# Scheduling a two-layer linear-attention and Mish kernel as one block on a more detailed timing simulator

## The chip, the cores and the metric

The kernel runs on one NeuronCore of a Trainium2 chip. Its time is the device time of one execution in microseconds, and a version is judged by the median of its runs. The engines are called as in the profile: PE is TensorE's matmul stream and PEld its weight loads, DVE is VectorE, ACT is ScalarE, POOL is GpSimd, and SP is the engine whose queue issues every DMA of this kernel.

## The reference

The input x has 2048 tokens of 640 features, in float32. Two layers are run one after the other with the same weights. Each layer has two parts, and each part adds its result to x:

```
x = x + A(layernorm(x))     # linear attention, 32 heads of 20 features
x = x + B(layernorm(x))     # dense 640 -> 1536, Mish, dense 1536 -> 640
x = x + A(layernorm(x))
x = x + B(layernorm(x))

A:  q, k, v = split(x @ wqkv)
    phi(z) = concat(softmax(z @ w_phi), softmax(-z @ w_phi))        # per head
    o = phi(q) @ (phi(k)^T v) / (phi(q) . sum_s phi(k) + 1e-6)
    return o @ wo
B:  h = x @ w1 + b1
    return (h * tanh(softplus(h))) @ w2
```

The sums over all tokens in phi(k)^T v separate each attention part into a first pass, which makes the sums, and a second pass, which uses them.

## The kernel before

Tokens are worked in 8 blocks of 256, each of two tiles of 128. Every large product is made in three passes of float32 matmuls: weights and activations are each cut into a high part (rounded to 12 bits) and the low rest, and high by high, high by low and low by high are summed in PSUM. The cut of a weight (`split`, L123 to L125) is a DMA into the staging tile `st`, of which there are two, a rounding copy on ScalarE (L124) and a subtraction (L125) on GpSimd or, for the values' weights, on VectorE.

Per layer there are three stages.

- `attend_first`: for each tile the products for keys, queries and values (`project`, L293), the softmax features in stages spread over ScalarE, VectorE and GpSimd (L314 to L325), the store of phi(q) to DRAM (L367), and the sums phi(k)^T v (L359). The next block is normalized and transposed meanwhile: `Transposed.step` makes transposes on TensorE (L252), a rounding copy on ScalarE and a subtraction on VectorE (L258).
- `attend_second`: phi(q) is loaded (L463) and transposed (L477); the transposes leave PSUM by ScalarE (L483) or VectorE (L481); the averages are made (L498) and divided (L507 to L511); they are transposed (L252) and multiplied by wo (L293), and the result is added to x (L518). In between, W1 and half of W2 are loaded and split.
- `dense`: a step takes 256 hidden features of one block: `hidden` makes 30 matmuls (L569) into one PSUM tile named `one`, `mish` runs its elementwise chain L582 to L595 over ScalarE and VectorE with its last subtraction on GpSimd (L595), and `contract` adds 24 matmuls (L611) into two PSUM tiles named `mm`. The trace order is skewed by two: `hidden` of step i comes before `contract` of step i - 2. A block has six steps; at a block's end `end` adds the result to x (L629). Near a block's end the next block's three transpose steps are traced around the last `hidden`.

PSUM holds four `one` tiles and two `mm` tiles. All five engines run queues in order; they wait for one another by semaphores.

The order in each queue is made at compile time. The framework runs the traced program through a timing simulator; whenever an engine can take an instruction in the simulation, it gets the ready one that was traced earliest, and PSUM and SBUF buffers are handed out in the same run. The chip then keeps that order, whatever the real times are. The kernel binds this choice in a few places: most ScalarE instructions outside `mish`, `split` and the transposes' copies are chained into trace order by a helper, and a few loads are told to be issued behind a named instruction. For instance:

```
def act(*args, **kw):
    ...
        with tc.issue_after(last_act[0]):
            ins = nc.scalar.activation(*args, **kw)
```

The framework has two timing simulators. The one in use before is the simpler one.

Of the kernel before, what the change touches and what calls it, by code (L numbers as in the profile page):

```python
# [16 lines left out]
P = 128  # L17
S = 2048
D = 640
F = 1536  # L20
H = 32
DH = 20
KD = D // P
KF = F // P
BT = 2
# [17 lines left out]
def kernel(  # L43
# [28 lines left out]
    def big_tile():  # L72
        return work.tile([P, EW], F32, tag="big", name="big", bufs=5)
# [7 lines left out]
    def row_block(t, b):  # L81
        return t[b * BLK:(b + 1) * BLK, :].rearrange("(p t) d -> p t d", t=BT)

    # constants
    ident = const.tile([P, P], F32, name="ident")
    make_identity(nc, ident)
    b1s = const.tile([P, KF], F32, name="b1s")
# [1 line left out]
    nc.vector.memset(neg_half, -0.5)  # L89
    two = const.tile([P, 1], F32, name="two")  # L90
    nc.vector.memset(two, 2.0)
    # per group of three heads: the block diagonal of phi_k^T [v | 1], by pairs of groups
    kvb = const.tile([120, GP, P], F32, name="kvb")
    # rstd and -mean*rstd of every token, for the next layer norm
    stats = const.tile([P, NB, 2, BT], F32, name="stats")

    # spills
    wp_d = dram.tile([2, 2, KD, P, D], F32, name="wp_d")
    e_d = dram.tile([NT, P, EW], F32, name="e_d")
    x1_d = dram.tile([S, D], F32, name="x1_d")  # L100
# [2 lines left out]
    last_act = [None]  # L103

    def act(*args, **kw):
        """An activation that ScalarE issues after the one before it in this order."""
        if last_act[0] is None:
            ins = nc.scalar.activation(*args, **kw)
        else:
            with tc.issue_after(last_act[0]):  # L110
                ins = nc.scalar.activation(*args, **kw)
        last_act[0] = ins.ins

# [1 line left out]
    def v_tile():  # L115
        return work.tile([P, VW], F32, tag="v", name="v", bufs=2)

# [9 lines left out]
    def r1_pair(k):  # L127
        return tuple(wts.tile([P, F], F32R, tag=f"r1{s}{k}", name=f"r1{s}{k}") for s in "hl")
# [8 lines left out]
        return tuple(wts.tile([P, D], F32R, tag=f"r2{s}{j}", name=f"r2{s}{j}") for s in "hl")  # L137

    def load_v_weights():
        """R1 holds [Wk' | Wv] by chunks of rows; the values' part."""  # L140
        ws = [r1_pair(k) for k in range(KD)]
        for k in range(KD):
            split(ws[k][0][:, D:2 * D], ws[k][1][:, D:2 * D], wv[k * P:(k + 1) * P, :], D, nc.vector,
                  (None, None, v_tile, v_tile, big_tile)[k])
        return ws
# [31 lines left out]
        return ws  # L177

    def load_w2(fs):
        """Rows of W2 by tiles of hidden features; the last five go where Wo was."""  # L180
        ws = {}
        for f in fs:
            ws[f] = r2_pair(f if f < 5 else (f + 5 if f < 7 else f - 2))
            split(ws[f][0], ws[f][1], w2[f * P:(f + 1) * P, :], D, nc.gpsimd)
        return ws

    def load_raw(which):
        """W's transpose, queries' or keys' part, by chunks of six heads."""
        raw = []
        wide = r2_wide(10 + which, F32)  # L190
        for t in range(6):
            rows = 120 if t < 5 else 40
            if t < 5:
                r = wts.tile([P, D], F32, tag=f"r2{'hl'[which]}{5 + t}", name=f"raw{which}{t}")
            else:
                r = wide[:, 0]
            nc.sync.dma_start(r[:rows], wqk_t[which * D + t * 120:which * D + t * 120 + rows, :])
            raw.append((r, rows))
        return raw

    def fold_phi(ws, bd, raw):
        """W' = W . blockdiag(w_phi), from W's transpose."""
        for k in range(KD):
            if k % 2:
                ps = [one_tile(), one_tile()]
            else:
                ps = mm_tile()
                ps = [ps[:, 0], ps[:, 1]]
            for t in range(6):
                r, rows = raw[t]  # L210
                nc.tensor.matmul(ps[t // 3][:, (t % 3) * 120:(t % 3) * 120 + rows],
                                 r[:rows, k * P:(k + 1) * P], bd[:rows, t, :rows],
                                 start=True, stop=True)
            hi, lo = ws[k][0][:, :D], ws[k][1][:, :D]
            for c, (a, b) in enumerate(((0, 360), (360, D))):
                nc.scalar.activation(hi[:, a:b], ps[c][:, :b - a], AF.Copy)
                nc.vector.tensor_tensor(lo[:, a:b], ps[c][:, :b - a], hi[:, a:b].bitcast(F32),
                                        op=ALU.subtract)

# [1 line left out]
    def norm_stats(t, xt):  # L221
        """Mean and variance of a tile's tokens."""
        bn = work.tile([P, 2, 6], F32, tag="bn", name="bn", bufs=4)
        for c in range(2):
            nc.vector.bn_stats(bn[:, c], xt[:, t, c * HC:(c + 1) * HC])
        mv = work.tile([P, 2], F32, tag="mv", name="mv", bufs=4)
        nc.vector.bn_aggr(mv, bn)
        return mv

    def norm_scale(b, mvs):  # L230
        """stats[:, b] = rstd, -mean*rstd."""
        ve = work.tile([P, BT], F32, tag="ve", name="ve", bufs=4)
        for t in range(BT):
            nc.gpsimd.tensor_scalar(ve[:, t:t + 1], mvs[t][:, 1:2], LN_EPS, 1.0, op0=ALU.add, op1=ALU.mult)
        nc.gpsimd.tensor_tensor(stats[:, b, 0], ve, neg_half, op=ALU.pow)
        for t in range(BT):
            nc.vector.scalar_tensor_tensor(stats[:, b, 1, t:t + 1], mvs[t][:, 0:1], -1.0,
                                           stats[:, b, 0, t:t + 1], op0=ALU.mult, op1=ALU.mult)

    class Transposed:  # L240
        """A block's rows, transposed: chunks of features by tokens, high and low parts."""

        def __init__(self, rows):
            self.rows, self.hs, self.ls = rows, [], []
# [24 lines left out]
        return work.tile([P, D], F32, tag="xn", name="xn", bufs=2)  # L269

    def normed(b, xt):
        """The normalized block, yet to be transposed."""
        xn = [row_tile() for _ in range(BT)]
        for t in range(BT):
            act(xn[t], xt[:, t, :], AF.Identity,
                                 bias=stats[:, b, 1, t:t + 1], scale=stats[:, b, 0, t:t + 1])
        return Transposed(xn)

# [1 line left out]
    def project(xts, t, ws, col, ps=None):  # L280
        """(tokens of tile t) . w[:, col:col + D], in halves."""
        if ps is None:
            mm = mm_tile()
            ps = [mm[:, 0], mm[:, 1], mm]
# [10 lines left out]
        return ps  # L295

    def both(ps):
        """The two halves as one operand, where they lie in one tile."""
        return ps[2][:, :, :HC]

# [1 line left out]
    def query_tile(i):  # L302
        return r2_wide(10 + i % 2, F32).rearrange("p s d -> p (s d)")

    def features(ps, e, pool_sub):
        """Softmax of both signs, [head, sign, feature], in stages."""
        eg = e.rearrange("p (g d) -> p g d", d=DH)
        eh = e.rearrange("p (h s d) -> p s h d", s=2, d=DH)
        act(e.rearrange("p (c h s d) -> p s c h d", c=2, s=2, d=DH)[:, 1],
# [18 lines left out]
    def fetch(x_src, b, xt=None):  # L328
        xt = x_tile() if xt is None else xt
        nc.sync.dma_start(xt, row_block(x_src, b))  # L330
        return xt

    def attend_first(layer, x_src, first):
        """Sums phi_k^T [v | 1] over all tokens; spills phi_q."""

        def fetch_normed(b):
            xt = fetch(x_src, b)
# [94 lines left out]
        return kva, kvz, o_ws, advance  # L432

    def finish_kv(kva, kvz, mask):
        """The block diagonals of the sums, features on partitions, by pairs of groups."""
        acc, acz = (work.tile([P, D], F32, tag="st", name="st", bufs=2) for _ in range(2))
        for src, dst, p1, n, w in ((kva, acc, P, 4, 120), (kvz, acz, P, 1, 120), (kvz, acz, 42, 1, 80)):
            c = 120 if w == 80 else 0
# [14 lines left out]
    def attend_second(x_src, x_dst, acc, at, begin_next):  # L453
# [11 lines left out]
            return ins  # L465

        def features_t(b):
            """phi_q transposed, by pairs of groups of three heads."""
            es = loaded.pop(b)
            phs = []  # L470
            for m in range(6):
# [13 lines left out]
            return phs  # L485

        def averages(phs):
            """phi_q . phi_k^T v over phi_q . sum(phi_k), a block's rows."""
            os_ = []
            for t in range(BT):  # L490
                po = mm_tile()
# [59 lines left out]
                at(b)  # L551
        return nxt

# [1 line left out]
    def dense(x_src, x_dst, w1s, w2s, first, last):  # L555
        blocks = {0: first}
        exps = [None]
# [17 lines left out]
            return ah, al  # L575

        def mish(pr, js, ph, ta, tb, ah, al):
            """n = e^h (e^h + 2); mish = h n / (n + 2)"""
            part = lambda t, c: t[:, c * 512:(c + 1) * 512].rearrange("p (f s) -> p f s", f=2)[:, js]
            e, n, r, m = part(ta, 0), part(ta, 1), part(tb, 0), part(tb, 1)  # L580
            for j in range(js.start, js.stop):
# [88 lines left out]
                    end(b)  # L670
        return nxt, kv_ws

    src, first = x, None
    for layer in range(LAYERS):
        last = layer == LAYERS - 1
        dst = out if last else x2_d
        acc = attend_first(layer, src, first)
        if layer == 0:
            nc.sync.dma_start(b1s, b1)
        w1s = []  # L680
        w2s = {}

        def at(b):
            if b < KD:
                w1s.append(r1_pair(b))
                split(w1s[b][0], w1s[b][1], w1[b * P:(b + 1) * P, :], F, nc.gpsimd)
            else:
                w2s.update(load_w2(((0, 1, 2), (3, 4), (5, 6))[b - KD]))

        x1t = []  # L690

        def begin_dense():
            x1t.append(fetch(x1_d, 0, big_tile().rearrange("p (t d) -> p t d", t=BT)))
            return normed(0, x1t[0])

        begun = attend_second(src, x1_d, acc, at, begin_dense)
        first = dense(x1_d, dst, w1s, w2s, [x1t[0], begun, None], last)
        src = dst


# [36 lines left out]
```

## Time and profile before

| | |
|---|---|
| median of 3 runs | 1491.22 us (1490.75 to 1491.38) |
| span of the profiled execution | 1497.6 us |
| TensorE matmul busy | 1461.3 us, 98%, 12100 matmuls |
| VectorE busy | 985.0 us, 66% |
| ScalarE busy | 623.8 us, 42% |
| GpSimd busy | 455.7 us, 30%, 360 instructions |
| DMA | 135.37 MB, mean 90 GB/s |

The profile is of one execution, and no other time of that execution is given than its span, which is 6.4 us (0.4%) above the median of the runs. Busy times are taken from the span's records. In the chain of waits and in the groups, "A <- B" says that instruction A waited last for instruction B. In the tables of stretches, PEclk is the share of TensorE's full clock that was granted in that stretch.

### The profile page before, as it was taken

What the parts mean: (1) busy time and instruction counts of PE and PEld (TensorE: products, weight loads), DVE (VectorE), ACT (ScalarE), POOL (GpSimd) and SP (SyncE); (2) the same over time, 40 slices, a digit from 0 to 9 for tenths busy, and PEclk for the clock granted to TensorE, in tenths of its full rate; (3) what the DMA queues carried; (4) which work ended last, traced back from release to release, by engine and by line L of the source; (5) the groups of instructions that cost most, each with busy time, mean ns of one, the idle gap of its engine ahead of it and who ended that gap; (6) DMA issues with size and microseconds to landing.
All of it is one profiled execution on the core that took longest, in us unless ns stands there. A gap on an engine that the chain in (4) does not pass through costs nothing.

```text
span 1497.6 us, 28601 instructions
## 1 busy us (share of the span) xinstructions
PE 1461.3 (98%) x12100; PEld 1438.8 (96%) x12100; DVE 985.0 (66%) x1734; ACT 623.8 (42%) x1051; POOL 455.7 (30%) x360
## 2 busy tenths in 40 slices
PE   7999999999999999999989999999999999999998
PEld 7999999898999999999989999998999999999998
DVE  5787767655577667666659566675656776666665
ACT  4534343523354444444444344333334444444443
POOL 1554434424042222122144334352332212111111
PEclk9999999999999999999999999999999999999999
DMA  8521113665310110001441112136562000000100
GB/s 264 198 76 54 71 62 117 219 234 199 116 45 18 36 36 31 7 36 36 161 174 71 54 54 88 55 109 251 206 202 89 10 18 37 36 36 36 36 2 36
DMA packets 39586, 135.37 MB, mean 90 GB/s; under 512 B 4777, under 2 KB 6313, under 8 KB 39457
## 3 DMA queue, kind: packets, MB, share of 16 engines
q1 hardware_dynamic: 39457, 133.53, 25.2%
q8 instruction: 95, 1.56, 0.4%
q14 instruction: 34, 0.28, 0.1%
HBM read 85.02 MB, written 48.50 MB: 89 GB/s over the span
## 4 chain that ended last, share of the span: by engine, by line
PE 80%; DVE 7%; DMA 4%; ACT 3%; POOL 2%; issue 1%; SPq 0%; DVEq 0%; ACTq 0%; POOLq 0%
PE mm L293 33%; PE one L569 19%; PE mm L611 19%; PE one L252 3%; DMA st<-in_w 3%; PE one L359 3%; PE one L477 2%; DVE big L593 1%; PE mm L498 1%; DVE big L585 1%; DVE big L584 1%; DVE big L592 1%; POOL r2l L125 1%; DVE big L591 1%; ACT big L586 1%
## 5 line engine op out<-in xcount | busy, mean ns | idle before, releaser
L611 PE MATMUL mm<-r2h,ol 128*128 128x320 f32 x1280 | 304.7, 311 | 6.2 <-POOL ol L595 5.2
L595 POOL TENSOR_TENSOR ol<-big,ol 128x512 fp32r<-128x512 f32 (+1 forms) x98 | 129.7, 1324 | 494.2 <-ACT ol L594 386.9
L569 PE MATMUL one<-xtl,r1h 128*128 128x256 f32 x960 | 271.8, 283 | 1.0 <-DVE xtl L258 1.0
L569 PE MATMUL one<-xth,r1h 128*128 128x256 f32 x960 | 272.7, 284 | 0.0
L569 PE MATMUL one<-xth,r1l 128*128 128x256 f32 x960 | 271.6, 283 | 0.0
L611 PEld LDWEIGHTS mm<-r2h,ol 128*128 128x128 f32 x1280 | 221.2, 190 | 7.3 <-POOL ol L595 6.0
L293 PE MATMUL mm<-r2h,xth 128*128 128x320 f32 x640 | 202.2, 316 | 0.0
L611 PE MATMUL mm<-r2l,ol 128*128 128x320 f32 x640 | 198.8, 311 | 0.0
L293 PE MATMUL mm<-r2h,xtl 128*128 128x320 f32 x640 | 198.2, 310 | 0.0
L293 PE MATMUL mm<-r2l,xth 128*128 128x320 f32 x640 | 198.2, 310 | 0.0
L293 PE MATMUL mm<-r1h,xth 128*128 128x320 f32 x600 | 188.8, 315 | 0.0
L293 PE MATMUL mm<-r1h,xtl 128*128 128x320 f32 x600 | 185.4, 309 | 0.0
L293 PE MATMUL mm<-r1l,xth 128*128 128x320 f32 x600 | 185.3, 309 | 0.0
L569 PEld LDWEIGHTS one<-xtl,r1h 128*128 128x128 f32 x960 | 183.9, 192 | 1.4 <-DVE xtl L258 1.4
L569 PEld LDWEIGHTS one<-xth,r1l 128*128 128x128 f32 x960 | 184.2, 192 | 0.0
L569 PEld LDWEIGHTS one<-xth,r1h 128*128 128x128 f32 x960 | 183.8, 191 | 0.0
L584 DVE TENSOR_SCALAR big<-big 128x512 f32<-128x512 f32 (+1 forms) x98 | 56.2, 574 | 162.1 <-ACT big L582 157.9
L594 ACT ACTIVATE ol<-big 128x512 fp32r<-128x512 f32 (+1 forms) x98 | 61.0, 623 | 199.0 <-DVE big L593 198.9
L325 POOL TENSOR_TENSOR r<-r,r 128x1280 f32<-128x1280 f32 x32 | 75.7, 2365 | 155.4 <-DVE r L324 154.0
L586 ACT ACTIVATE big<-big,two 128x512 f32<-128x512 f32 (+1 forms) x98 | 70.0, 715 | 125.9 <-DVE big L585 123.8
L293 PEld LDWEIGHTS mm<-r2h,xth 128*128 128x128 f32 x640 | 120.8, 189 | 0.8
L611 PEld LDWEIGHTS mm<-r2l,ol 128*128 128x128 f32 x640 | 121.4, 190 | 0.0
(107 smaller groups left out, 2937.8 us busy)
## 6 DMA issues: line engine op xcount, KB each, us to landing
e_d<-r SPq DMA_DIRECT2D x32, 640.0 KB, 3.2
big<-e_d SPq DMA_DIRECT2D x32, 640.0 KB, 6.4
xt<-x_d SPq DMA_DIRECT2D x30, 640.0 KB, 4.0
x_d<-xt SPq DMA_DIRECT2D x23, 640.0 KB, 2.9
st<-in_w SPq DMA_DIRECT2D x44, 320.0 KB, 3.8
xt<-in_x SPq DMA_DIRECT2D x16, 640.0 KB, 5.0
out<-xt SPq DMA_DIRECT2D x6, 640.0 KB, 2.9
st<-in_wo SPq DMA_DIRECT2D x10, 320.0 KB, 3.0
```

What stands on the lines that cost most here:

```text
L125: eng.tensor_tensor(lo[:, c0:c1], st, hi[:, c0:c1].bitcast(F32), op=ALU.subtract)
L252: nc.tensor.transpose(ps[:, c, t * P:(t + 1) * P], self.rows[t][:, (c0 + c) * P:(c0 + c + 1) * P], ident)
L293: nc.tensor.matmul(ps[c][:, :HC], l[:, sl], r, start=(n == 0), stop=(n == 3 * KD - 1))
L325: nc.gpsimd.tensor_tensor(eg, eg, r.unsqueeze(2).to_broadcast([P, 2 * H, DH]), op=ALU.mult)
L359: nc.tensor.matmul(acc[64 * n:64 * n + m, c:c + w], v[:, GW * g:GW * g + m], e[:, 120 * g:120 * g + w], start=(i == 0 and p in (0, 4)), st ...
L477: nc.tensor.transpose(ps[:rows, n, t * P:(t + 1) * P], es[t][:, 120 * g:120 * g + rows], ident)
L569: nc.tensor.matmul(ph[:, j, :], l, r, start=(n == 0), stop=(n == 3 * KD - 1))
L584: nc.vector.tensor_scalar_min(e, e, E_CAP)
L586: nc.scalar.activation(r, n, AF.Ln, bias=two)
L594: nc.scalar.activation(ah[:, js], n, AF.Copy)
L595: nc.gpsimd.tensor_tensor(al[:, js], n, ah[:, js].bitcast(F32), op=ALU.subtract)
L611: nc.tensor.matmul(pys[t][:, c, :HC], l[:, j, sl], r, start=(f == 0 and n == 0), stop=(f == KF - 1 and n == 2))
```

## The change

The two-layer loop is put inside a block of its own, and the block is marked to be scheduled with the more detailed of the framework's two timing simulators. The setup ahead of it (the identity, two small constants, the table preload and the declarations of buffers) stays outside and is scheduled as before. What is traced in the block is scheduled as a unit, and nothing outside is mixed in. By the framework's description of the option, the simpler simulator leaves out the fixed cost of GpSimd's elementwise instructions, which the detailed one has. No instruction is added, removed or resized, and no buffer count changes. Comments and docstrings are taken out as well.

```
-    src, first = x, None
-    for layer in range(LAYERS):
-        last = layer == LAYERS - 1
-        dst = out if last else x2_d
-        acc = attend_first(layer, src, first)
...
-        begun = attend_second(src, x1_d, acc, at, begin_dense)
-        first = dense(x1_d, dst, w1s, w2s, [x1t[0], begun, None], last)
-        src = dst
+    with tc.block(schedule_with_timeline_sim=True):
+        src, first = x, None
+        for layer in range(LAYERS):
+            last = layer == LAYERS - 1
+            dst = out if last else x2_d
+            acc = attend_first(layer, src, first)
...
+            begun = attend_second(src, x1_d, acc, at, begin_dense)
+            first = dense(x1_d, dst, w1s, w2s, [x1t[0], begun, None], last)
+            src = dst
```

## The prediction

> **What bounds the kernel now.** I read the page's busy times first, then TensorE's list of waits, then ScalarE's, then the order of time around each long wait. The page:
>
> ```profile
> span 1497.6 us, 28601 instructions
> PE 1461.3 (98%) x12100; PEld 1438.8 (96%) x12100; DVE 985.0 (66%) x1734; ACT 623.8 (42%) x1051; POOL 455.7 (30%) x360
> ```
>
> TensorE does the same 12100 matmuls after the change, so the change can only move the 36.3 us of the span in which no matmul is busy, and what clock is lost around them. TensorE's waits (line, what it waited for, total us, times, longest):
>
> ```profile
> PE mm L211 <- DMA raw<-in_wqk_t: 7.6, 1, 7.6
> PE one L252 <- DVE xn L511: 6.5, 14, 2.9
> PE mm L611 <- POOL ol L595: 5.2, 3, 4.2
> PE one L477 <- ACT ol L483: 4.2, 3, 2.5
> PE one L252 <- DVE big L589: 3.8, 2, 1.9
> PE mm L611 <- DVE big L629: 1.0, 1, 1.0
> PE one L569 <- DVE xtl L258: 1.0, 2, 0.5
> ```
>
> With 2.5 us in smaller rows the list holds 31.8 us; the other 4.5 us is nearly all the end after the last matmul. The 7.6 us is the first load and the end is the last store; no order removes them. That leaves 24.2 us. Two stretches then run at half clock, which the stretches show (columns: stretch, length, busy times, PEclk, DMA):
>
> ```profile
> 1024.50:1027.00 2.50, 2.50 (x10) 2.50 (x11) 1.50 (x6) 0.42 (x1) 0.92 (x2) 0.50 0.60 171
> 759.00:764.00 5.00, 5.00 (x19) 5.00 (x20) 0.52 (x1) 0.74 (x1) 2.00 (x2) 0.50 0.02 8
> ```
>
> The second follows a gap of 4.56 us from matmul to matmul (at 754.25); 21 matmuls took some 267 ns in place of 147, which costs 21 x 0.12 = 2.5 us. The first follows a gap of 3.12 us at 1021.39; its 30 matmuls of one product took 5.81 us where others take 4.64, so 1.2 us. A gap of 2.78 us at 359.99 was followed by none. The pool that any order can win is thus 24.2 + 3.7 = 27.9 us, 1.9% of the time. Whoever looks for a larger gain must find it outside TensorE's waits, and there is nothing there.
>
> **The steady stretches.** From 468 to 740 us and from 1200 to 1480 us TensorE never pauses. In step 20 of the first dense stage GpSimd's L595 ends at 557.88 and its matmul starts at 563.66: 5.8 us in hand. The two L595 forms take 0.723 us (shortest, 256 elements) and 1.296 us (median, 512), so 2.2 ns an element and about 0.15 us fixed (an estimate from these two). The description says that the simpler simulator omits just this fixed cost; all 360 instructions together make 54 us by it, but 0.15 us against 5.8 us moves no order there. I cost the steady stretches at nothing; the cover is those 5.8 us, and were it gone, each of some 90 steps would pay its excess. What can change lies at the transitions.
>
> **The change part by part.** It adds, removes and resizes no instruction. It moves them in their queues, SP's DMAs included, and it opens a block.
>
> *The block's entry.* No jump shows in this trace. Bound: zero if each engine runs straight on; one instruction packet if it must fetch, and 95 packets on the instruction queue took 0.4% of 16 engines' span, so 1.0 us each. SP issues the first load at 0.72 us and TensorE's first matmul waits for loads, so nothing hides it. I take the middle, +0.5. The Trainium skill (Runtime: NRT & Kernel Launch, Instruction fetch mechanics) says that a taken branch to code outside the fetched window stalls for that fetch; by it the term would be +1.0. No jump is in this trace to test it.
>
> *Weight copies at the head of ScalarE.* ScalarE's waits:
>
> ```profile
> ACT r1h L124 <- DMA st<-in_w: 72.5, 23, 8.0
> ACT r2h L124 <- DMA st<-in_w: 26.3, 10, 8.5
> ```
>
> and the order of time on ScalarE around 360 (start, length, in brackets the idle time before and what ended it):
>
> ```profile
> 360.41 0.74 ACT L124 ACTIVATE r2h<-st 128x640 fp32r<-128x640 f32 x1 [3.22 <-DMA st<-in_w]
> 362.14 2.04 ACT L483 ACTIVATE ol<-one 120x512 f32<-120x512 f32 x4
> ```
>
> The simulated order put L124 where its load should have landed; on the chip it had not, and ScalarE stood 3.2 us with four ready L483 behind it. TensorE's L477 then waited 2.5 us for a PSUM tile. The same shape stands at 1099 (1.5 us) and at 1018.9 to 1020.8, where a waiting L124 holds back an xth copy and TensorE loses 2.9 us and 1.2 us of clock. A simulator that times DMAs more closely would let the chain go first: 4.0 + 4.1 = 8.1 us gone. What is late next is L124, by one or two copies of 0.74 us; its weights are used a stage later.
>
> *A transpose ahead of ready matmuls.* At 435.95 TensorE stands before the last two L252 of the next block, which wait for a PSUM tile until L589 has read it:
>
> ```profile
> 435.95 0.28 PE L569 MATMUL one<-xth,r1l 128*128 128x256 f32 x1
> 438.13 0.44 PE L252 MATMUL one<-ident,xn 128*128 128x128 f32 x2 [1.90 <-DVE big L589]
> 438.32 1.12 PE L611 MATMUL mm<-r,ol 128*128 128x320 f32 x6
> ```
>
> The 24 matmuls L611 behind them were ready: their L595 ended at 436.16. Chosen by real readiness they go first, and L252 falls into them. Again at 1173.85. Gone: 3.8 us, and the 1.0 us that L569 then waits for L258. In the wait for L629 (1.0 us) I see no ready work for certain, and leave it.
>
> *The end of the first layer.* The 4.25 us before L611 at 754.56 come from L595:
>
> ```profile
> L595 POOL TENSOR_TENSOR ol<-big,ol x98: 723/1296/4906, 412.7 to 1489.9; 128x512 fp32r<-128x512 f32 x94, 128x256 fp32r<-128x256 f32 x4
> ```
>
> (Of GpSimd's L595: shortest, median and longest in ns.) The shorter form takes 0.723 us elsewhere and 4.906 us here, at 753.85, while VectorE runs eight instructions with two inputs nearly without pause (five splits L125 and three of `mish`). The Trainium skill (SBUF — State Buffer, Summary: rules for kernel authors) says that a VectorE instruction with two SBUF inputs and a GpSimd instruction exclude one another until the first ends. By that rule L595 would wait for one of them (0.83 us) and not for all; a scheduler that follows it believes L595 done by 755.4, keeps TensorE's order, and the gap stays; the trace disagrees with the rule, since all eight went first. If instead values' matmuls (L293) are drawn into the gap, 4.25 + 2.5 = 6.8 us go. I take 0, the value of today's row, and keep 6.8 for the range.
>
> *The rest.* Thirteen waits for L511 in the second pass make 3.6 us without the long one; both `mm` tiles are then held by the averages, so they stay.
>
> *New waits.* A greedy order tuned by another clock makes its own mistakes: hand-set chains stay while their neighbours move. Nothing in the trace prices them but today's mistakes of the same sort: 8.1 + 4.8 = 12.9 us. Bounds: 0 and about twice that; I take half, 6.5.
>
> Sum: 0.5 - 8.1 - 4.8 + 6.5 = -5.9 us. Against the span that gives 1491.7; the profiled span stands 6.4 us above the median, so 1485.3 for the median (0.4% faster).
>
> **Rivals.** *Tiles taken by running ahead* (slower). If the new order draws `hidden` ahead whenever `contract` isn't ready, the four `one` tiles fill, and the next block's transposes wait at each block end as they do at two of fourteen inside the dense stages today, for 1.9 + 0.5 = 2.4 us each. At ten more ends it costs 24 us, and with the 8.1 won (the 4.8 are not) and 0.5 for the entry that is +16.4: 1507.6. It decides from four ends, where it outweighs the 8.1. For it: the tiles are held for a whole `mish` chain. Against it: 5.8 us in hand in the steady state. Chance 0.39, with smaller forms down to 1495.
>
> *No change that shows.* The order in the large stretches is bound by PSUM tiles and data, and the two corrections are eaten by new mistakes: 0.5 - 12.9 + 12.9, so 1491.7. Chance 0.13. (A measurement of this kernel tells 0.2%, 3 us, from no change.)
>
> *The layer's end filled as well.* -5.9 - 6.8 = -12.7: 1478.5. Chance 0.14, part of faster.
>
> *The option does little because the simulators agree.* It falls together with the second rival, since the queue order would be the same.
>
> **How the numbers follow.** Forecast -5.9 has 0.34, the filled end 0.14: faster 0.48. Same 0.13. Slower 0.39. Low end: everything won and no new waits would be 0.5 - 12.9 - 6.8 = -19.2, so 1472.0; I stop at 1475. High end: the first rival at ten ends, 1507.6, so 1508. The likeliest case's own range is 1478 to 1490.
>
> **What would show it.** Right: the waits of L477 for L483 and of L252 for L589 leave TensorE's list; ScalarE's wait for `st` falls well under 72.5 us; the half-clock stretch at 1024 is gone; the steady stretches show no new pause. Wrong: TensorE's matmul idle over 40 us, with L252 waiting for L589 or L569 at many block ends, or a pause in a steady stretch; or a first matmul later than 9 us. Were TensorE's busy time itself to change by over 5 us, the premise that order alone moves would have failed.

## The result

The changed kernel is slower: 1500.85 us median of 4 runs (1499.31 to 1502.17) against 1491.30 us (1490.75 to 1493.1) for the kernel before on the same chip, a ratio of 1.0063 with a 95% interval of 1.0045 to 1.008. On another chip it was 1501.18 against 1496.07, 1.0035 (1.0021 to 1.0049). Forecast was 0.4% faster, 1485.3 us.

The profile after is of one execution, and so is each profile below. The run that left it took 1502.17 us, 2.1 us more than its span. First the page's span and busy times:

```profile
span 1500.1 us, 28643 instructions
PE 1467.2 (98%) x12100; PEld 1443.2 (96%) x12100; DVE 1014.7 (68%) x1734; ACT 618.7 (41%) x1051; POOL 455.0 (30%) x360
```

The same 12100 matmuls are busy 5.9 us longer, for two reasons that are read below: some ran at a lower clock, and in the second passes the same matmuls in a new order take longer. TensorE's waits (line, what it waited for, total us, times, longest):

```profile
PE one L252 <- DVE xn L511: 17.5, 14, 4.5
PE mm L211 <- DMA raw<-in_wqk_t: 7.6, 1, 7.6
PE mm L498 <- ACT ol L483: 1.0, 2, 0.6
PE mm L611 <- ACT ol L594: 0.8, 2, 0.4
```

The waits for L589, L595, L629 and L258's wait in the dense stages are all gone. One row of before has grown instead, from 6.5 to 17.5 us: the transposes of the averages in the second attention pass wait for VectorE's division L511, 14 times as before, seven in each pass. The waits of TensorE come to less than before, 28 us against 32. To see why the time is longer, I cut each trace at the first average L498 and the first matmul L569 of each layer (the first block's transposes L477 are thus counted ahead of the second pass). The profiled execution of before had caught an unusually long wait at the first layer's end, so the second column is another execution of the same kernel (its run is the first experiment):

| us | before | before, run again | after |
|---|---|---|---|
| start and first pass, layer 1 | 276.3 | 276.5 | 276.2 |
| second pass, layer 1 | 126.1 | 124.7 | 135.0 |
| dense, layer 1, and first pass, layer 2 | 609.9 | 605.3 | 597.7 |
| second pass, layer 2 | 128.0 | 128.9 | 136.5 |
| dense, layer 2 | 353.1 | 353.1 | 350.2 |
| from the last matmul's end | 4.3 | 4.3 | 4.6 |
| span | 1497.6 | 1492.7 | 1500.1 |

Against the second column the dense stages and what follows them gain 7.6 + 2.9 = 10.5 us, and the two second passes lose 10.2 + 7.7 = 17.9 us.

**The steady loss: 0.87 us a block.** A steady block of the second pass took 15.48 us from its first L477 to the next block's, and now takes 16.35 us. TensorE's order of time in one block, of before and then of after (start, length, instruction, its count, in brackets the idle time before it and what ended it):

```profile
311.91 2.56 PE L477 MATMUL one<-ident,big 128*120 128x128 f32 x22
314.40 2.77 PE L498 MATMUL mm<-kvb,ol 120*64 120x63 f32 x88
317.42 0.41 PE L252 MATMUL one<-ident,xn 128*128 128x128 f32 x2 [0.24 <-DVE xn L511]
```

```profile
318.74 2.35 PE L477 MATMUL one<-ident,big 128*120 128x128 f32 x20
321.02 0.68 PE L498 MATMUL mm<-kvb,ol 120*64 120x63 f32 x16
321.63 0.41 PE L477 MATMUL one<-ident,big 128*80 128x128 f32 x2
321.98 2.35 PE L498 MATMUL mm<-kvb,ol 120*64 120x63 f32 x72
325.11 0.41 PE L252 MATMUL one<-ident,xn 128*128 128x128 f32 x2 [0.78 <-DVE xn L511]
```

Two things differ. The averages L498 begin before the last two transposes L477, and the stretch from the first L477 to the last L498's end takes 5.59 us and not 5.26. And the gap behind it is 0.78 us and not 0.24. The second comes from the order inside the 88 matmuls. There are 44 for each of the two tiles, and they start in pairs, 22 for a tile; a pair is called a wave here. Before, all 22 waves of tile one came first. Now the program's queue has 4 waves of tile one, 4 of tile two, the two L477, then again 4 and 4, 12 of one, 1 of two, 2 of one, 13 of two. Tile one's last average stands 13 waves from the end and not 22. VectorE's L507, L508 and L511 for tile one (some 1.5 us) start behind it, and its cover has shrunk by 9 waves of 0.06 us. Together that is 0.33 + 0.54 = 0.87 us for a steady block. Fourteen such blocks would make 12.2 us; the experiments below put the two passes' loss from it at 9.9 us. Not every block is a steady one: the pass's second block takes 18.1 us with the new order against 17.8 with the old one bound (from the runs with the copies chained), so it loses 0.3 us and not 0.87.

**The loss at the first block of each pass.** The gap ahead of L252, counted from the start of the last matmul to the start of the next as all gaps between matmuls below, is 3.86 us at 286.08 and 4.69 us at 1018.68. ScalarE's order of time there, then VectorE's:

```profile
286.75 0.74 ACT L124 ACTIVATE r1h<-st 128x640 fp32r<-128x640 f32 x1 [2.75 <-DMA st<-in_w]
287.39 0.85 ACT L111 ACTIVATE xth<-one 128x512 fp32r<-128x512 f32 x2
```

```profile
285.41 0.26 DVE L507 TENSOR_SCALAR den<-mm 128x24 f32<-128x24 f32 x2 [0.68 <-PE mm L498]
288.00 0.69 DVE L258 TENSOR_TENSOR xtl<-one,xth 128x512 fp32r<-128x512 f32 x1 [2.34 <-ACT xth L111]
288.61 0.35 DVE L508 RECIPROCAL den<-den 128x32 f32<-128x32 f32 x1
288.87 0.36 DVE L258 TENSOR_TENSOR xtl<-one,xth 128x256 fp32r<-128x256 f32 x1
289.15 0.88 DVE L511 TENSOR_TENSOR xn<-mm,den 128x480 f32<-128x480 f32 x2
```

Read from the bottom: L511 stands behind L258 in VectorE's queue, L258 waits for the copy L111 on ScalarE, and L111 stands behind a rounding copy L124 of W1 that waits 2.75 us for its load. TensorE waits for the end of that chain. Its clock is then low for 19 matmuls L293 (and 21 at 1023.7), as two stretches show (busy times, PEclk, DMA share, GB/s):

```profile
289.90:297.00 7.10, 7.06 (x32) 7.09 (x33) 1.53 (x6) 1.15 (x2) 2.99 (x3) 0.60 0.42 129
1023.30:1030.00 6.70, 6.63 (x27) 6.66 (x28) 1.30 (x4) 1.16 (x2) 2.28 (x2) 0.55 0.40 120
```

At 0.267 us in place of 0.147 these 40 matmuls cost 4.8 us. That isn't all added, since half clock cost 3.7 us in the first profile of before as well (2.5 us of it at the first layer's end). In the two second passes alone matmuls are busy 252.9 us against 243.2 in both profiles of before, 9.6 us more; 14 blocks times the 0.33 us above make 4.6 us of that, and the added half clock most of the rest. Before, a gap of this shape stood only at the second layer (3.1 and 3.7 us in its two profiles).

**The gain.** At the end of the first block of each dense stage matmuls L611 now stand between the eighth transpose and the last two, 24 of them directly behind the eighth (that row is the first of them), and the last two no longer wait:

```profile
433.96 1.04 PE L252 MATMUL one<-ident,xn 128*128 128x128 f32 x8
434.76 0.54 PE L611 MATMUL mm<-r2h,ol 128*128 128x320 f32 x2
...
444.88 0.38 PE L252 MATMUL one<-ident,xn 128*128 128x128 f32 x2
```

At the first layer's end matmuls L293 of the next stage begin at 758.75 among the last L611, and no wait is left there.

### The profile page after: what moved, and what is told of

Its sections match the earlier page's. It is cut to its first block, busy times and chain, and to the rows that moved or that the text cites. A ratio compares the mean times of both kernels' runs of the same rounds, so it can differ in the third digit from the quotient of the medians.

```text
span 1500.1 us, 28643 instructions
## 1 busy us (share of the span) xinstructions
PE 1467.2 (98%) x12100; PEld 1443.2 (96%) x12100; DVE 1014.7 (68%) x1734; ACT 618.7 (41%) x1051; POOL 455.0 (30%) x360
## 4 chain that ended last, share of the span: by engine, by line
PE 92%; DMA 3%; DVE 3%; ACT 1%; issue 1%; POOL 0%; SPq 0%; DVEq 0%; ACTq 0%
PE mm L293 36%; PE mm L611 22%; PE one L569 22%; PE one L252 4%; PE one L359 2%; PE one L477 2%; DMA st<-in_w 2%; PE mm L498 2%; PE one L293 1%; DMA st<-in_wv 1%; DVE xn L511 1%; DVE big L591 1%; PE mm L211 0%; DVE den L508 0%; PE one L211 0%
## 5 line engine op out<-in xcount | busy, mean ns | idle before, releaser
L611 PE MATMUL mm<-r2h,ol 128*128 128x320 f32 x1280 | 302.4, 309 | 0.8 <-ACT ol L594 0.8
L595 POOL TENSOR_TENSOR ol<-big,ol 128x512 fp32r<-128x512 f32 (+1 forms) x98 | 129.0, 1316 | 488.7 <-ACT ol L594 408.7
L569 PE MATMUL one<-xth,r1h 128*128 128x256 f32 x960 | 272.5, 284 | 0.0
L569 PE MATMUL one<-xth,r1l 128*128 128x256 f32 x960 | 271.6, 283 | 0.0
L569 PE MATMUL one<-xtl,r1h 128*128 128x256 f32 x960 | 271.6, 283 | 0.0
L611 PEld LDWEIGHTS mm<-r2h,ol 128*128 128x128 f32 x1280 | 219.2, 188 | 1.3 <-ACT ol L594 1.3
L293 PE MATMUL mm<-r2h,xth 128*128 128x320 f32 x640 | 204.0, 319 | 0.0
L293 PE MATMUL mm<-r2l,xth 128*128 128x320 f32 x640 | 199.9, 312 | 0.0
L293 PE MATMUL mm<-r2h,xtl 128*128 128x320 f32 x640 | 199.8, 312 | 0.0
L611 PE MATMUL mm<-r2l,ol 128*128 128x320 f32 x640 | 197.6, 309 | 0.0
L293 PE MATMUL mm<-r1h,xth 128*128 128x320 f32 x600 | 188.8, 315 | 0.0
L293 PE MATMUL mm<-r1h,xtl 128*128 128x320 f32 x600 | 185.4, 309 | 0.0
L293 PE MATMUL mm<-r1l,xth 128*128 128x320 f32 x600 | 185.3, 309 | 0.0
L569 PEld LDWEIGHTS one<-xth,r1l 128*128 128x128 f32 x960 | 184.1, 192 | 0.0
L569 PEld LDWEIGHTS one<-xtl,r1h 128*128 128x128 f32 x960 | 183.9, 192 | 0.0
L569 PEld LDWEIGHTS one<-xth,r1h 128*128 128x128 f32 x960 | 183.8, 192 | 0.0
L584 DVE TENSOR_SCALAR big<-big 128x512 f32<-128x512 f32 (+1 forms) x98 | 79.4, 810 | 134.3 <-ACT big L582 134.1
L586 ACT ACTIVATE big<-big,two 128x512 f32<-128x512 f32 (+1 forms) x98 | 70.1, 715 | 162.4 <-DVE big L585 162.1
L293 PEld LDWEIGHTS mm<-r2h,xth 128*128 128x128 f32 x640 | 122.3, 191 | 0.9
L293 PEld LDWEIGHTS mm<-r2l,xth 128*128 128x128 f32 x640 | 122.3, 191 | 0.0
```

The lines of the kernel that those rows point to most:

```text
L293: nc.tensor.matmul(ps[c][:, :HC], l[:, sl], r, start=(n == 0), stop=(n == 3 * KD - 1))
L569: nc.tensor.matmul(ph[:, j, :], l, r, start=(n == 0), stop=(n == 3 * KD - 1))
L584: nc.vector.tensor_scalar_min(e, e, E_CAP)
L586: nc.scalar.activation(r, n, AF.Ln, bias=two)
L595: nc.gpsimd.tensor_tensor(al[:, js], n, ah[:, js].bitcast(F32), op=ALU.subtract)
L611: nc.tensor.matmul(pys[t][:, c, :HC], l[:, j, sl], r, start=(f == 0 and n == 0), stop=(f == KF - 1 and n == 2))
```

## The experiments

Three sets on three chips, each beside the kernel before on the same chip (1494.73, 1496.07 and 1495.69 us median there). Times in us:

| kernel | median | ratio to before (95%) | steady block of second pass |
|---|---|---|---|
| before, run again | 1494.51 (one run) | | 15.48 |
| block alone | 1498.39 | 1.0019 (0.9997 to 1.0041) | 15.48 |
| before, averages alternating | 1523.42 | 1.0181 (1.0162 to 1.02) | 16.64 and more |
| after, averages bound | 1492.29 | 0.9983 (0.997 to 0.9995) | 15.49 |
| after, run again | 1501.18 | 1.0035 (1.0021 to 1.0049) | 16.34 |
| after, only tiles ordered | 1496.73 | 1.0011 (0.9996 to 1.0026) | 15.76 |
| before, copies chained | 1493.26 | 0.9976 (0.9958 to 0.9994) | 15.69 |
| after, averages bound, copies chained | 1480.20 | 0.9898 (0.9877 to 0.9919) | 15.49 |
| after, copies chained | 1490.24 | 0.9957 (0.9941 to 0.9973) | 16.35 |
| before, both bindings | 1492.47 | 0.9973 (0.9957 to 0.9989) | 15.7 |
| after, both bindings, run again | 1479.47 | 0.9888 (0.9857 to 0.9919) | 15.48 |
| before, step moved at two block ends | 1501.71 | 1.0037 (1.0021 to 1.0053) | 15.48 |

**Before, run again** (no edit).

> The kernel before, unchanged, profiled once more. Its first profiled execution had a span of 1497.6 us while its runs take 1491.3; the changed kernel's runs lie 2 us above their spans. Theory A: the 4.56 us gap before L611 at the end of the first layer and the half clock after it (7 us together) came by chance in that one execution; then the span is near 1489 us and the gap is gone. Rival B: the gap is in every execution and the profile adds the rest; then the span is again near 1497 us with the same gap.

Its span is 1492.7 us. At the first layer's end TensorE's largest gap was 1.45 us, in place of 4.56:

```profile
756.59 0.42 PE L611 MATMUL mm<-r2h,ol 128*128 128x320 f32 x1 [1.14 <-ACT ol L594]
```

With the same queues, the long wait behind L595 was chance. The L595 in question (256 elements) took 4.91 us there and 0.97 here, where VectorE's L591 beside it took 0.96 us in place of 0.42: here VectorE was held up, there GpSimd. Over the seven profiles under the simpler simulator it took 4.90 to 4.91 us in three and 0.96 to 0.97 in four; over the seven under the detailed one it took 2.37 to 2.40 in each. A comparison of after with the first profile of before alone would have credited the change with it.

**Block alone.** The block without the option, so the simpler simulator orders it:

```
-    with tc.block(schedule_with_timeline_sim=True):
+    with tc.block():
```

> The changed kernel with the block kept but scheduled by the simpler simulator. Theory: the whole difference comes from the order that the detailed simulator picks, so this is the time before, 1489 to 1494 us, with the averages made tile by tile (22 and 22 matmuls). Rival: opening a block costs by itself (an entry of 1 us or more, or buffers freed later); then 1494 us or more, and the first matmul later than 7.6 us.

No difference shows: the interval takes in 1, though its upper end leaves room for 0.4%, and the steady block is as before. The order of the block alone differs from before only at the start: some 50 of TensorE's 12100 matmuls change places, all in the first 26 us, and no compute engine's order differs behind 100 us. So the option, not the block, makes the order that is read above.

**Before, averages alternating.** The kernel before, with the loops over tiles and over groups of heads exchanged, so that the two tiles' averages alternate:

```
-            for t in range(BT):
-                po = mm_tile()
-                for g in range(G):
+            pos = [mm_tile() for _ in range(BT)]
+            for g in range(G):
+                for t in range(BT):
+                    po = pos[t]
...
```

> The kernel before, simpler simulator, no block; the averages' loops exchanged, so that the two tiles' matmuls alternate group by group. Theory: the first tile's sum is then finished 20 matmuls (0.6 us) later against the end of all, so each of 14 blocks waits 0.8 to 0.9 us for L511 in place of 0.25: 9 us more, 1498 to 1503 us. Rival: only the last transposes' place between the matmuls costs, not the interleaving; then 1490 to 1493 us.

The direction is right and the size is beyond what was expected: 27 us over before, with 26.1 us of waits of L252 for L511 (14 times). In a steady block TensorE now stands idle for 1.41 us:

```profile
321.93 0.41 PE L252 MATMUL one<-ident,xn 128*128 128x128 f32 x2 [1.41 <-DVE xn L514]
```

(L514 is L511 in this source.) With strict alternation tile one is ready one group before the end and nearly the whole VectorE chain is bare. The steady blocks make some 16 of the 27 us (14 times 1.16); most of the rest is in the passes' last blocks, whose cause isn't shown. The order of these matmuls alone, on the old simulator, is enough to make the kernel slower.

**After, averages bound.** The changed kernel, with the averages issued behind the block's last L477, and tile two's behind tile one's:

```
+                        tr[0] = nc.tensor.transpose(ps[...], ...).ins     (L477)
...
+            after = tr[0]
             for t in range(BT):
...
+                        with tc.issue_after(after):
                             num[0] = nc.tensor.matmul(po[...], ...)
+                after = num[0]
```

> The changed kernel, with the averages' matmuls told to be issued behind the block's last transpose, and the second tile's behind the first tile's; all else still ordered by the detailed simulator. Theory: interleaving the two tiles' averages costs 0.87 us a block (period 16.35 in place of 15.48), so 14 blocks give back 12 us: 1486 to 1491 us, and the waits of L252 for L511 fall from 0.78 to about 0.25 us. Rival: the period is longer for another reason (the copies, the DMAs); then 1497 to 1503 us.

The steady block is back, 22 transposes and then 88 averages (lines are 1 to 4 higher in this source: L478, L501 and L515 are L477, L498 and L511). Its transposes L252 wait as in before:

```profile
321.31 0.41 PE L252 MATMUL one<-ident,xn 128*128 128x128 f32 x2 [0.25 <-DVE xn L515]
```

The gaps at the passes' first blocks stayed (2.39 and 4.14 us), so these have another cause. With them the time is 1 us over the range that was expected.

**After, run again** (no edit), as the level of the second set.

> The changed kernel once more, as the level against which the others of this set are read. Theory (the order inside the second pass's averages costs about 10 us, and the layer's start there about as much again): 0.5 to 0.8% over the kernel before, block period in the second pass 16.35 us, 14 waits of L252 for L511 of 0.7 to 0.9 us each. Rival (the first profile caught chance stalls): under 0.3% over, and a period below 16 us.

Steady block 16.34 us, gaps of 3.59 and 4.62 us at the first blocks, 14 and 19 matmuls at half clock behind them: the losses recur. The ratio came out below the expected 1.005 and above the rival's 1.003: after took the same time as on the first chip (1501.18 and 1500.85 us), and before's median was 5 us higher here.

**After, only tiles ordered.** Tile two's averages behind tile one's; the last L477 may still fall in between:

```
+            after = None
             for t in range(BT):
...
+                        with tc.issue_after(after) if after else nullcontext():
                             num[0] = nc.tensor.matmul(po[...], ...)
+                after = num[0]
```

> The changed kernel, where only the second tile's averages (L498) are bound to issue behind the first tile's; the block's last transposes may still fall between. Theory (the loss is that the first tile finishes 13 instead of 22 matmuls before the block's end, and the chain L507, L508, L511 is then exposed): the waits of L252 for L511 fall from 0.78 to about 0.25 us, a gain of 0.53 x 14 = 7.5 us; the other 0.33 us a block (the stretch of L477 and L498 itself) stays if it comes from the split of the transposes: period about 15.8 us, time 7 to 9 us below the changed kernel. Rival (the split of the transposes is what costs): period stays above 16.1 us and the time falls by under 4 us.

```profile
322.04 0.45 PE L501 MATMUL mm<-kvb,ol 120*64 120x63 f32 x8
322.42 0.41 PE L478 MATMUL one<-ident,big 128*80 128x128 f32 x2
...
325.55 0.41 PE L252 MATMUL one<-ident,xn 128*128 128x128 f32 x2 [0.25 <-DVE xn L515]
```

The exposure is 0.25 us again, and the split of the transposes alone keeps 0.28 us a block (15.76 against 15.48). That separates the two parts of the 0.87 us as expected. The time fell by 4.4 us, less than the 7 to 9 expected: near the passes' ends L478 waited 2.6 us and L501 1.7 us for ScalarE, gaps that after did not have.

**Before, copies chained.** The kernel before, with the copies L124 that `at` traces in the second pass put into the trace-order chain of ScalarE:

```
-            nc.scalar.activation(hi[:, c0:c1], st, AF.Copy)
+            copy(hi[:, c0:c1], st, AF.Copy)
...
-                split(w1s[b][0], w1s[b][1], w1[b * P:(b + 1) * P, :], F, nc.gpsimd)
+                split(w1s[b][0], w1s[b][1], w1[b * P:(b + 1) * P, :], F, nc.gpsimd, copy=act)
```

> The kernel before (simpler simulator, no block) with the same copies L124 put into ScalarE's trace order chain. Tests the prediction's step on the weight copies by itself: by it the gaps near 360, 1021 and 1099 us go and 4 to 8.1 us are gained (0.3 to 0.5%). Rival (the copies wait inside the chain, and the chain's later work behind them): no gain, or slower by the length of the waits, with ScalarE's waits for st in the place of the gaps.

The three gaps of before at 360, 1021 and 1099 us are gone, but the medians differ by 2.8 us only, below the 4 to 8.1 that the prediction's step gives; the ratio gives 0.24%, and its interval, 0.06% to 0.42% or 0.9 to 6.3 us, reaches into that range. TensorE's order is the same as before, matmul by matmul. A steady block now takes 15.69 us, 0.21 more, all of it in its transposes (22 L477 in 2.77 us and not 2.56), which gives back 2 to 3 us. The step has the right sign here and, with that added, about two thirds of its size.

**After, averages bound, copies chained.** Both edits on the changed kernel.

> The changed kernel with the averages bound behind the block's last transpose and tile two behind tile one, and, new here, the rounding copies L124 of W1 and of half of W2 put in the second pass into ScalarE's trace order chain, so that none can stand ahead of the chain's earlier work. Theory (the gaps of 2.4 and 4.1 us with half clock behind the second, at the first blocks of the second passes, come from a copy L124 that waits for its load at the head of ScalarE): the gaps go, and with them some 8 us of the first pinned version: 12 to 20 us below the changed kernel in all. Rival (the copy only waits elsewhere in the chain, with the same weight): within 3 us of the first pinned version, 8 to 11 us below the changed kernel, with ScalarE's waits of L124 still ahead of TensorE's gaps.

1480.2 us, 1% below before and 21 us below after. TensorE's two largest waits (the first is at the start, the second in the second passes):

```profile
PE mm L211 <- DMA raw<-in_wqk_t: 7.5, 1, 7.5
PE one L252 <- DVE xn L515: 5.0, 14, 0.8
```

No gap over 1.3 us is left, and TensorE's idle time is 20.8 us of the span, against 32.9 in after.

**After, copies chained.** The second edit alone on the changed kernel.

> The changed kernel with only the copies L124 of the second pass put into ScalarE's trace order chain; the averages stay interleaved. Theory (the two losses of the second pass are separate): the first blocks' gaps of 3.6 and 4.6 us shrink to the 0.8 us of the other blocks and the 14 to 21 matmuls at half clock behind them go, 6.6 + 4.2 = some 11 us below the changed kernel, with the block period still at 16.35 us. Rival (the interleaving makes the copies' waits harmful, and either repair removes both): the period falls too, and the time comes to within 4 us of the version with both bindings, some 1480 us.

1490.24 us, some 11 us below after (the ratios 0.9957 and 1.0035 differ by 0.78%), as the theory of two separate losses gives. TensorE's order is that of after, matmul by matmul, so the gain comes from the copies' place on ScalarE and from what moves with it (DMAs, subtractions on GpSimd, 32 instructions on VectorE). The first blocks' gaps are gone, no half clock is left, and the steady block still has its 16.35 us:

```profile
303.71 0.41 PE L252 MATMUL one<-ident,xn 128*128 128x128 f32 x2 [0.78 <-DVE xn L511]
```

The second passes read the two losses apart (layer 1, then 2): after 135.0 and 136.5 us, with the copies chained 129.4 and 129.3, with both bindings 124.8 and 124.0. The copies cost 5.6 + 7.2 = 12.8 us and the averages' order 4.6 + 5.3 = 9.9 us. Both are costs in after; what before paid for its copies is set against the first below.

**Before, both bindings.** The simpler simulator without the block, with the same two edits.

> The simpler simulator without the block, but with both bindings of the best version so far (averages behind the block's last transpose, tile two behind tile one; copies L124 of the second pass in ScalarE's chain). Theory (the detailed simulator's order is worth its corrections in the dense stages: 3.8 us of L252 for L589, 1.0 of L569 for L258, the waits of L611, and half clock behind some of these): 6 to 10 us slower than the same bindings on the detailed simulator, with the waits of L252 for L589 back. Rival (all of the best version's gain is in the bindings): within 3 us of it.

1492.47 us: on the same chip the detailed simulator is worth 13.0 us with the same bindings. More than the expected 6 to 10; 2 to 3 us of it are the steady block, 15.7 us here against 15.48, and the rest is in the dense stages and what follows them (605.7 and 353.9 us here, 597.6 and 350.2 there). The order here is, on every compute engine, that of before with the copies chained: binding the averages changes nothing under the simpler simulator, which had them so already. Among the waits that the detailed simulator's order removes are:

```profile
PE one L252 <- DVE big L593: 3.8, 2, 1.9
PE mm L615 <- POOL ol L599: 1.8, 4, 0.8
```

(L593, L599 and L615 are L589, L595 and L611.)

**After, both bindings, run again.**

> The changed kernel with both bindings, beside the others of this set. Expected as before: 0.8 to 1.2% below the kernel before, PE idle about 21 us, no matmul gap over 1.3 us.

1479.47 us (1479.15 to 1481.52). It is the fastest version measured. No gap is over 1.3 us, and TensorE is idle for 20.5 us.

**Before, step moved.** The kernel before; at the first block's end of each dense stage the third transpose step is traced between the two halves of `contract`:

```
-                if pr == n_pr - 1 and (b + 1 < NB or not last):
+                if pr == n_pr - 1 and b and (b + 1 < NB or not last):
                     nxt.step()
...
+                if half and (t, j) == (1, 0):
+                    half()                     # nxt.step for the first block
```

> The kernel before, where at the end of the first block of each dense stage the third transpose step (L252) is traced between the two tiles' halves of contract (L611) and no longer ahead of it. By the prediction's step the two waits of L252 for L589 (1.9 us each) and of L569 for L258 (0.5 us each) go: 4.8 us below the kernel before. Rival (TensorE then waits elsewhere, for L258 of the moved step or for the L611 operands): no more than 2 us.

A miss: 6 us slower than before. The waits of L252 for L589 left TensorE's list, but the step's copy of xth went behind L586 in ScalarE's queue, and that stands behind the chain of `mish`. ScalarE's order of time, and TensorE's:

```profile
444.56 0.72 ACT L586 ACTIVATE big<-big,two 128x512 f32<-128x512 f32 x1 [1.79 <-DVE big L585]
445.19 0.36 ACT L111 ACTIVATE xth<-one 128x256 fp32r<-128x256 f32 x1
```

```profile
445.61 0.58 PE L569 MATMUL one<-xth,r1h 128*128 128x256 f32 x1 [2.71 <-ACT xth L111]
```

Two gaps of 2.99 us, each with 11 or 12 matmuls at half clock behind it, took the place of two of 2.2 us. Moving the step by hand isn't what the detailed simulator's order does: that one draws matmuls L611 ahead of `hidden`'s and leaves the last two transposes where their tile is free.

## Why the prediction was wrong, by its steps

Two steps failed. *Weight copies at the head of ScalarE* had the wrong sign: 8.1 us were to be won, and some 8.0 were lost. *The rest* was put at nothing, and the averages' order cost 9.9 us there. Against the second profile of before the terms as measured are 0 for the entry, +8.0, -10.5 and +9.9, in all +7.4 us, which is what the two spans differ by (1500.1 and 1492.7); forecast was -5.9. The range reached up to the time only for a mechanism that didn't come, the first rival's.

*The block's entry* (+0.5): SP issues the first load at 0.72 us as before, and the first matmul starts at 7.65 us, between the 7.55 and 7.70 of the two profiles of before, so nothing shows. The Trainium skill (Runtime: NRT & Kernel Launch, Instruction fetch mechanics) speaks of a stall at a taken branch out of the fetched window, by which the term would have been 1.0; no such stall shows in this trace, and whether the block's entry is such a branch it doesn't tell.

*Weight copies at the head of ScalarE* (-8.1): the mechanism, a copy that waits for its load at the head of ScalarE, is the right one; that the new order would take the copies out of the way was wrong. The waits of L477 for L483 left the list, 4.2 and 3.4 us in the two profiles of before. But ScalarE's waits of L124 for `st` in the same rows fell only from 98.8 to 94.0 us, and one of them moved to a worse place, the first block of the first layer's pass, where a gap of 3.86 us and 2.3 us of clock appeared; the second layer's gap grew from 3.73 to 4.69 us. The second passes give the sum: the copies cost 12.8 us after (above), and before they cost, by an estimate, the 4.8 us by which its two second passes stand over those of the version with both bindings (253.6 and 248.8 us). Chaining the copies in before took these to 251.8, with some 2.5 us given back in the transposes, which fits. So this term was some +8.0 us and not -8.1. That a better simulator would see the loads' landing was an assumption about the simulator, and no row of the trace bore on it.

*A transpose ahead of ready matmuls* (-4.8): right. The two rows, 3.8 and 1.0 us, are gone, and matmuls L611 stand where the prediction put them.

*The layer's end* (0, with 6.8 as a rival) and the wait for L629 (left): both went, as the rival said, with matmuls L293 drawn in. The stages hold -10.5 us in all, so this step and the transposes were together 5.7 us better than forecast. The price of 6.8 us was itself too high, since it was read from an execution with a chance wait: 4.56 us there, 1.45 in another execution of the same kernel. Of the 4.9 us between the two spans of before, 4.6 are in the stretch that holds this wait. The prediction's reading of the long L595, that GpSimd let all eight VectorE instructions go first, is thus of one execution; in another it was VectorE that waited.

*The rest* (0): this step failed by leaving a cost out. It said that the waits for L511 stay because the averages hold both `mm` tiles. They did stay, 14 of them, but each has a length that depends on the order inside the 88 matmuls, and that order was free: both tiles' averages are ready in turn and nothing binds them. It cost 9.9 us, more than the whole forecast gain. The prediction counted only the dense stages' stretches as steady; but the second pass's blocks repeat as well, 14 of them, and the prediction looked for new orders only in the dense stages and at transitions.

*New waits* (+6.5): the right idea, sized too low. The new losses in the second passes are the 17.9 us of the two terms above (8.0 + 9.9), inside the bounds of 0 and about 26; a quarter of the upper one was taken, for want of a place. The place of the 9.9 could be found in the kernel: two PSUM tiles, filled by matmuls of one kind with nothing between them that orders them, and a VectorE chain behind the first.

The rival that ends slower named the `one` tiles at the dense stages' ends. That did not happen. Slower came by the second pass, so the 0.39 on slower stood on another mechanism.

Why the detailed simulator begins the averages before the last transposes isn't shown. It hands out the earliest traced ready instruction, so in its run the last L477 should have been not yet ready when the first waves of averages were; on the chip, in before and with the binding, 22 L477 run without a pause. That its ScalarE or VectorE times for emptying PSUM are longer than the chip's would explain it, and no run here tests that.

## What to carry to other kernels

When a scheduler is exchanged, look first at the loops that repeat most and ask in each what orders instructions of equal readiness: an order that was only a habit of the old scheduler, here "all of tile one, then tile two", is a property of the kernel that must be written down if an engine's chain hides behind it. A new scheduler's gains and losses come together and can be separated: with two bindings that restore what had been luck, the one that lost 0.35 to 0.63% gained 1.0 to 1.1%, while the same bindings under the old one gained 0.3%, all by the copies. And before comparing two profiles, run the old kernel's profile twice: the gap of 4.56 us that was 1.45 in the next execution would have passed for a third of the effect here.

## What the runs showed of the hardware

The half clock behind a gap isn't decided by its length alone. Over all profiles here, each of 18 gaps in the matmuls of 2.98 to 4.84 us (2.7 to 4.6 us of them idle) was followed by 9 to 21 matmuls at half clock. Of 14 gaps of 2.16 to 2.79 us (those that end at L477 or L498 left out), three were: one of 2.79 us, and two of the twelve of 2.16 to 2.21 us that stand ahead of the same two transposes L252. Two gaps that end at L498 (1.88 and 2.15 us) were followed by it too, by the granted clock. The Trainium skill (TensorE: Matmul & The Clock Gate, Why this matters for your kernels) advises against idle gaps above about 3 us; the 18 gaps agree with it, and the others show that shorter ones can cost as well. Near the start a gap of 1.21 us (at 17.8 us, six profiles of changed kernels) was followed by 10 to 19 slow matmuls in three; these three had a further gap of 0.72 to 1.10 us ahead of it (it ends at 15.7 to 15.9 us), which the other three lack, so it isn't the same gap six times.

The records of the granted clock show how it goes down: between the first and the last matmul there are 26 stretches at 0.50 in the 14 profiles, and each is 3.41 or 6.83 us long. Such a stretch began up to 2.9 us ahead of its gap's end or up to 1.5 us behind it, so more or fewer matmuls fell into it. The same page of the Trainium skill (What's actually happening) says that the window is free-running and the count varies from run to run, which agrees with these differing places and counts.

The times of before scattered by 9 to 11 us on the three later chips (19 to 23 executions on each; 1490.01 to 1501.25 us on the first), while the version with both bindings stayed within 2.9 us on each of two (4 executions each; 1479.15 to 1482.25 over both). After stayed within 2.9 us as well (4 and 7 executions), with its waits on the copies' loads, and with the averages bound it scattered by 7 us (10 executions). So neither the copies nor the simulator alone accounts for the scatter, and its cause wasn't tested.
